# Clustered attention and two MoE layers on one core: the copy's mask in PSUM, V's peak and split in other steps, and attention's last ten steps regrouped

## The chip, the core and the metric

The kernel runs on one core of a Trainium2 chip. The metric is the device time of one execution in microseconds (us), of which the median of several runs is given. The engines are TensorE (PE in the profile, PEld its weight loads), VectorE (DVE), ScalarE (ACT), GpSimd (POOL) and SyncE (SP), which here issues the DMAs.

## The reference

Attention with clusters, 2 batches of 8 heads, 768 tokens, 64 values a head, then two feed-forward layers over 1536 tokens. A query sees a key only where both are nearest to the same of 16 centroids. A query with no key in its cluster has only equal scores, so it gets the mean of V.

```python
q_assign = np.argmax(np.einsum('bhsd,hcd->bhsc', q_n, c_n), axis=-1)
k_assign = np.argmax(np.einsum('bhsd,hcd->bhsc', k_n, c_n), axis=-1)
mask = q_assign[:, :, :, None] == k_assign[:, :, None, :]
scores = np.where(mask, scale * np.matmul(q, k.transpose(0, 1, 3, 2)), -1000000000.0)
attn = np.exp(scores - np.max(scores, axis=-1, keepdims=True))
x = np.matmul(attn / (np.sum(attn, axis=-1, keepdims=True) + 1e-09), v)   # heads side by side: 1536 x 512
...
h = x @ w_in      # 512 -> 2048
g = np.where(h >= 1, h, np.where(h <= -1, 0.0, (h + 1) ** 2 / 4))
x = g @ w_out     # 2048 -> 512
...
h = x @ w2_in
out = (s * np.maximum(h, 0) ** 2 + b) @ w2_out
```

## The kernel before, in words

**Precision by halves.** Products are taken with each operand split in a high part and a low part, so that a product is three matmuls (high by high, low by high, high by low). Every tensor that goes to TensorE has a pair of instructions that splits it: a rounding copy on ScalarE, and a subtraction on VectorE or GpSimd. V is first scaled by a power of two, taken from its largest magnitude, and split in two halves of 16 bits.

**Attention in steps.** The 16 heads are 8 pairs; a head has 6 chunks of 128 keys, which makes NS = 96 steps. `slot(t)` writes one step:

- two matmuls of row maxima (`max_mm`, L722) for chunk t + 9, in two banks of PSUM called m, and VectorE's reduces of them (L733);
- `scores` (L783, L784) of chunk t, in three banks called s, and `probs`: two exponentials a half on ScalarE (L794, L795) and the low half pl by a subtraction (L797) on GpSimd, or on VectorE for the steps that the table VPL names;
- `values` (L813) of chunk t − 2, 18 matmuls into the one bank called o. After a head's sixth chunk `finish` (L824, L828, L831) reads that bank on VectorE, and only then the next head's values can start;
- the pieces that tables have put into step t: `steps` hold triples (TensorE part, ScalarE part, VectorE part) whose TensorE part stands at the end of step t and whose other parts stand in step t + 1; `mid` stands before the step's values, `extra` at its end, `dmas` at its start.

The pieces are the turns of q and k (transposes L483, L492, L496), the clusters (L520 to L565), V's magnitudes (`scale_v`, L595), V's peak (`peak_row` L607 to L617, `peak_all` L628 to L642), V's split (`split_v` on ScalarE, L650; `split_v2` on VectorE, L654), the mean of V (L666 to L672), the row of maxima (`max_row`, L762, L767, and a DMA L771 that the scores of that head need), the stacks that DMAs build from the halves (L683), the replacement of unmatched rows (`no_match`, L838 on ScalarE, then the predicated copy L839 on VectorE) and the transposed output (`x_out`, L855, L860, L863, two pieces a pair). All that need a bank in PSUM take it from the pool x by `spare()`. The pool has two banks, given out by turns, so a piece waits until the readers of the last piece but one are done.

**Order.** Each engine runs its instructions in the order in which the program was written, so the tables set it. With z = 12p for pair p, the table PV gives the steps (relative to z) of V's load, `scale_v`, `peak_row`, `peak_all`, and of the four splits, for even and odd pairs apart. V has one buffer in SBUF (rv), so the load of a pair waits until the last `split_v2` of the pair before has read it. The DMAs queue on SP in order.

**Into the MoE.** After attention 96 units follow, each of twelve matmuls for h (L241), the activation (L254 to L270), the split of g (L275, L277) and twelve matmuls for y (L302) into four banks that `emit_y` names by pools. Their weights arrive as 64-bit numbers and are converted: L134 on ScalarE, four operations on VectorE (L151, L155, L159, L163), then L179 on ScalarE and L180 on GpSimd. The first four pieces of weights are converted in attention's last ten steps, at times that the table EARLY gives (and a pool of the intermediate buffers), and h of the first two units is computed there or right behind (`early_h`).

Of the kernel before, what the change touches and what calls it, by code (L numbers as in the profile page):

```python
# [8 lines left out]
F32 = mybir.dt.float32  # L9
# [16 lines left out]
def clustered_attention_moe_kernel(  # L26
# [29 lines left out]
    J = S // 128  # L56
# [12 lines left out]
    NWA, NWB, NWC, NWD = 2, 5, 7, 2  # L69

    EARLY = (
        (85, 87, 87, 88, 88, 89, "m"), (88, 90, 90, 91, 91, 92, "m"), (91, 93, 93, 94, 94, 95, "x"),
        (95, 98, 98, 99, 99, None, "x"),
    )
    LOADS = (56, 62, 68)
    PACES = ((2, 0.7), (28, 0.9))
    TAIL = 3
    VPL = (87, 90, 93, 95)
    PV = ((-11, -9, (-8, -6), -5, -3, -3, -2), (-13, -11, (-8, -6), -5, -3, -2, 0))
    PX = ((7, 16, 17), (7, 16, 17))  # L80
    PT = (38, 35, 36, 34, 27, 26, 25, 24)
    PG = (23, 22, 20, 18, 17, 16, 14)
    PN = (8, 12, 9)


# [15 lines left out]
    def bank(kind, name):  # L101
        return banks[kind].tile([128, TB], F32, tag=kind, name=name)
# [81 lines left out]
    ff = {"wa": wa}  # L184
# [13 lines left out]
    units = [(m, t, c) for m, t, a, b in RUNS for c in range(a, b)]  # L198
# [16 lines left out]
    def w_free(m, c):  # L215

        x = w_pool(m, c)
        i = SHARES[x].index((m, c)) - {"wa": NWA, "wb": NWB, "wc": NWC, "wd": 0}[x]
        if x == "wd":
            return use2[0, FC - 1] + 1  # L220
        return use2[SHARES[x][i]] if i >= 0 else -2
# [5 lines left out]
    g_t, y_t, h_t = {}, {}, {}  # L227
# [56 lines left out]
    def emit_y(m, t, c):  # L284
        wh, wl = w_t[m, c][:, 0], w_t[m, c][:, 1]
        gh, gl = g_t.pop((m, t, c))
        begin, end = (m, t, c) in BEGIN, (m, t, c) in END
        if begin:
            y_t[m, t] = [bank(x, "y") for x in "mmxo"]
        y = y_t[m, t]  # L290
        order = [(i, n) for n in range(3) for i in range(KD)]
        if begin or end:
            order.sort()
        for i, n in order:
            cs = slice(i * 128, (i + 1) * 128)
            ws = slice(DM + i * 128, DM + (i + 1) * 128)
            wd = slice(DM, 2 * DM)
            if m == 0:
                ops = ((wh[:, ws], gh), (wh[:, ws], gl), (wl[:, ws], gh))
            else:  # L300
                ops = ((gh[:, cs], wh[:, wd]), (gl[:, cs], wh[:, wd]), (gh[:, cs], wl[:, wd]))
            nc.tensor.matmul(  # L302
                y[i], lhsT=ops[n][0], rhs=ops[n][1], start=(begin and n == 0), stop=(end and n == 2)
            )
        if end:
            emit_out(m, t, c, y_t.pop((m, t)))
# [50 lines left out]
    h = 3  # L357
    for n, w in enumerate(loadq[len(early):]):
        start, pace = PACES[w[0]]
        n -= (0, 2 * FC - len(early))[w[0]]  # L360
        h = max(h + 1.4, 2 * (w_free(*w[0:2]) + 3), 2 * (start + pace * n))
# [45 lines left out]
    def attention(es, prep):  # L407
        def pool(name, bufs, stack=es):
            side = "left" if stack is prep else "right"
            return stack.enter_context(tc.tile_pool(name=name, bufs=bufs, side=side))  # L410
# [10 lines left out]
        smp = pool("smp", 4)  # L421
# [23 lines left out]
        def spare():  # L445

            if spares:
                spares.append(spares.pop(0))
                return bank(spares[-1], spares[-1] + "b")
            return bank("x", "xb")  # L450
# [101 lines left out]
        def match(g, n):  # L552

            j0, j1 = PIECE[n]
            cs = slice(j0 * 128, j1 * 128)
            st = {}

            def pe():
                ps = st["ps"] = spare()[:, 0:(j1 - j0) * 128]
                nc.tensor.matmul(ps, lhsT=firsts, rhs=sims[g, "t"][:, cs], start=True, stop=True)  # L560

            def dve():
                if n == 0:
                    ohts[g] = ohp.tile([128, S], F32, tag="oht", name="oht")
                nc.vector.tensor_scalar(  # L565
                    out=ohts[g][:, cs], in0=st["ps"], scalar1=level[:, 0:1], scalar2=level[:, 1:2],
                    op0=ALU.is_gt, op1=ALU.mult,
                )

            return pe, None, dve  # L570
# [218 lines left out]
        def probs(t):  # L789
# [3 lines left out]
            for qs, ps in pr[t]:  # L793
                nc.scalar.activation(out=ph[:, qs], in_=ps, func=ACTF.Exp, scale=qk_scale)  # L794
                nc.scalar.activation(out=pf[:, qs], in_=ps, func=ACTF.Exp, scale=qk_scale)  # L795
            eng = nc.vector if t in VPL else nc.gpsimd
            eng.tensor_tensor(out=pl, in0=pf, in1=ph, op=ALU.subtract)  # L797
# [36 lines left out]

        def no_match(p):

            nm = smp.tile([128, 2, J], F32, tag="nm", name="nm", bufs=2)
            nc.scalar.activation(out=nm, in_=heads.pop((p, "mx")), func=ACTF.Relu, scale=-1.0, bias=low)  # L838
            nc.vector.copy_predicated(  # L839
                out=heads[p, "x"],  # L840
                mask=nm.bitcast(I32).rearrange("p h j -> p j h")[:, :, :, None].to_broadcast([128, J, 2, D]),
                data=vt[p][4][:, None].to_broadcast([128, J, 2, D]),
            )
# [54 lines left out]
        NS = NH * J  # L898
        steps, extra, mid, dmas = {}, {}, {}, {}

        def at(d, t, f, *a):
            d.setdefault(t, []).append((f, a))

        def step(t, x):
            steps.setdefault(t, []).append(x)

        for g in range(1, NH // 4):
            z = 24 * g
            for a, at_load, places in ((0, 46, PT[0:4]), (1, 34, PT[4:8])):
                p = 2 * g + a  # L910
                at(dmas, z - at_load, load_qk, p)
                for o, (nm, n) in zip(places, (("q", 0), ("q", 1), ("k", 0), ("k", 1))):
                    step(z - o, turn(p, nm, n))
            step(z - PG[0], sim(g, 0))
            step(z - PG[1] + int(g == 1), sim(g, 1))
            at(extra, z - PG[2], chain1, g)
            at(extra, z - PG[3], chain2, g)
            at(extra, z - PG[4], chain3, g)
            step(z - PG[5], match(g, 0))
            step(z - PG[6], match(g, 1))  # L920
        for p in range(NP):
            z = 12 * p
            zl, za, zs, zh, zg = PV[p % 2][0:3] + (PV[p % 2][3:5], PV[p % 2][5:7])
            at(dmas, z + zl, load_v, p)
            at(extra, z + za, scale_v, p)
            step(z + zs[0], peak_row(p))
            step(z + zs[1], peak_all(p))
            for e in range(2):
                at(extra, z + zh[e], split_v, p, e)
                at(extra, z + zg[e], split_v2, p, e)  # L930
            zx = PX[p % 2]
            step(z + zx[0], mean(p))
            if p < NP - 1:
                step(z + zx[1], x_out(p, 0))
                step(z + zx[2], x_out(p, 1))
# [11 lines left out]

        def early_h(n, kk):
            if kk == 0:
                ff["h"] = bank("m", "h")  # L950
            emit_h(*units[n], ff["h"], H_PARTS[3 * kk:3 * kk + 3])

        at(extra, 6 * (NH - 1) - 11, ready)
# [9 lines left out]
                at(extra, z[5], conv_split, w)  # L963
        for kk in range(KD):
            at(mid, NS - 5 + kk, early_h, 0, kk)
        at(extra, NS - 1, emit_g, *units[0], True)
        at(extra, NS - 1, emit_g2, *units[0], True)
        at(extra, NS, emit_split, *units[0], False)
        at(mid, NS, early_h, 1, 0)
        at(mid, NS + 1, early_h, 1, 1)  # L970
        at(extra, NS + 1, early_h, 1, 2)
# [164 lines left out]
```

## Time and profile before

| | |
|---|---|
| median of three runs | 797.81 us (797.04 to 799.7) |
| the profiled execution | 798.17 us |
| its span, first to last instruction | 796.5 us |
| mean granted TensorE clock | 0.981 |
| TensorE busy | 752.2 us (94%), 4993 matmuls |
| VectorE busy | 499.5 us (63%) |
| ScalarE busy | 472.7 us (59%) |
| GpSimd busy | 311.2 us (39%) |

A line of a timeline reads: start in us from the span's start, duration in us, engine, line of the kernel, operation, output and inputs by the program's names, sizes; in square brackets how long the engine had been idle before it, and what ended that. A line of the waits reads: the waiting engine and its line, the instruction that ended the waits, the total, how many, the longest. In the windows, the third number from the end is the granted clock, 1.00 being the full one; in front of it stand the busy us of TensorE, its weight loads, VectorE, ScalarE and GpSimd. Busy TensorE is not TensorE at its peak, since matmuls overlap in the pipeline.

### The profile page before, as it was taken

Reading aid. Unit: us, or ns where it says so; the run is one execution under the profiler, and the core shown is the slowest. Engines: PE = TensorE matmul, PEld = TensorE weight load, DVE = VectorE, ACT = ScalarE, POOL = GpSimd, SP = SyncE. Lnnn points to the kernel's source line nnn. Section 1 sums busy time; section 2 is a strip of 40 time slices with the busy share of each in tenths; the row PEclk is TensorE's granted clock in tenths of the full one; section 3 lists DMA queues with packets and bytes.
Section 4 is the critical chain, followed back from the end, with each engine's and each line's share of the span. In section 5 each row is a group of like instructions: output and inputs, shape, how many; then the busy total and the mean of one; then the engine's idle time right before and its main releaser. Section 6 shows DMA issues by size and latency. Waiting matters only on the chain.

```text
span 796.5 us, 13144 instructions
## 1 busy us (share of the span) xinstructions
PE 752.2 (94%) x4993; PEld 629.4 (79%) x4993; DVE 499.5 (63%) x878; ACT 472.7 (59%) x943; POOL 311.2 (39%) x237
## 2 busy tenths in 40 slices
PE   4799998998998799999999999999999999999998
PEld 3488887887886568788888888888888888888886
DVE  5779899898887696888447336879962322222222
ACT  4178968877898477787646425876653333343332
POOL 3057767767885346365405201654560000000000
PEclk9599999999999899999999999999999999999999
DMA  9576566536531144344203100443410100010001
GB/s 199 111 165 148 119 140 137 139 92 150 139 67 54 30 156 133 110 138 149 80 0 110 50 0 30 150 139 101 143 49 0 53 1 0 1 54 0 1 1 53
DMA packets 59887, 67.52 MB, mean 85 GB/s; under 512 B 29008, under 2 KB 47536, under 8 KB 59824
## 3 DMA queue, kind: packets, MB, share of 16 engines
q1 hardware_dynamic: 59824, 66.68, 31.8%
q8 instruction: 39, 0.64, 0.3%
q14 instruction: 24, 0.20, 0.1%
HBM read 43.03 MB, written 3.15 MB: 58 GB/s over the span
## 4 chain that ended last, share of the span: by engine, by line
PE 79%; DVE 14%; ACT 4%; issue 1%; DMA 0%; DVEq 0%; ACTq 0%
PE y L302 31%; PE h L241 30%; PE m L722 4%; PE o L813 4%; PE s L783 3%; PE s L784 3%; DVE rowmax L733 3%; PE xb L520 2%; DVE x L839 1%; PE xb L483 1%; DVE c L151 1%; PE xb L855 1%; DVE c L155 1%; DVE c L159 1%; DVE rowmax L754 1%
## 5 line engine op out<-in xcount | busy, mean ns | idle before, releaser
L241 PE MATMUL h<-xt_h,w 128*128 128x512 f32 x768 | 253.3, 391 | 1.7 <-ACT w L179 1.7
L797 POOL TENSOR_TENSOR pl<-pf,ph 128x768 f16<-128x768 f32 x92 | 155.3, 1693 | 93.8 <-ACT pf L795 71.1
L241 PEld LDWEIGHTS h<-xt_h,w 128*128 128x128 f32 x768 | 144.4, 188 | 32.2 <-ACT w L179 2.1
L241 PE MATMUL h<-xt_l,w 128*128 128x512 f32 x384 | 149.8, 390 | 0.0
L277 POOL TENSOR_TENSOR gl<-g,gh 128x512 fp32r<-128x512 f32 x51 | 66.8, 1310 | 187.1 <-ACT gh L275 187.1
L275 ACT ACTIVATE gh<-g 128x512 fp32r<-128x512 f32 x96 | 60.5, 630 | 108.3 <-PE y L302 66.7
L794 ACT ACTIVATE ph<-s 128x384 f16<-128x384 f32 x192 | 98.8, 515 | 32.7 <-PE s L784 31.1
L302 PE MATMUL y<-gh,w 128*128 128x512 f32 x384 | 109.8, 394 | 4.2 <-DVE g L268 2.8
L733 DVE TENSOR_REDUCE rowmax<-m 128x1 f32<-128x384 f32 x180 | 95.4, 549 | 24.2 <-PE m L722 23.0
L302 PE MATMUL y<-w,gh 128*128 128x512 f32 x384 | 105.3, 389 | 0.0
L795 ACT ACTIVATE pf<-s 128x384 f32<-128x384 f32 x192 | 100.2, 522 | 0.0
L270 DVE TENSOR_SCALAR g<-g,cols 128x512 f32<-128x512 f32 x48 | 27.4, 571 | 100.8 <-ACT g L261 100.6
L302 PEld LDWEIGHTS y<-gh,w 128*128 128x128 f32 x384 | 72.9, 190 | 20.9 <-DVE g L268 3.2
L180 POOL TENSOR_TENSOR w<-t,w 128x512 fp32r<-128x512 f32 x64 | 83.4, 1315 | 1.7 <-ACT w L179 1.7
L302 PEld LDWEIGHTS y<-w,gh 128*128 128x128 f32 x384 | 72.1, 188 | 15.0
L241 PEld LDWEIGHTS h<-xt_l,w 128*128 128x128 f32 x384 | 72.3, 188 | 14.6
L722 PE MATMUL m<-kb,qb 80*128 80x384 f32 x180 | 70.4, 395 | 7.3 <-DVE rowmax L733 6.9
L260 ACT ACTIVATE g<-h 128x512 f32<-128x512 f32 x48 | 28.6, 596 | 78.3 <-PE h L241 76.5
L813 PEld LDWEIGHTS <-ph 128*128 128x128 f16 x1152 | 55.2, 98 | 21.6 <-issue 13.4
L277 DVE TENSOR_TENSOR gl<-g,gh 128x512 fp32r<-128x512 f32 x45 | 31.2, 693 | 62.5 <-ACT gh L275 62.5
L813 PE MATMUL o<-vh,ph 128*128 128x65 f16 x576 | 63.9, 197 | 4.0 <-DVE x L831 3.8
L783 PE MATMUL s<-qa,ka 128*128 128x384 f32 x192 | 66.9, 349 | 0.0
(164 smaller groups left out, 1317.1 us busy)
## 6 DMA issues: line engine op xcount, KB each, us to landing
raw<-in_moe_w_in_dram SPq DMA_DIRECT2D x32, 512.0 KB, 5.2
raw<-in_moe_w_out_dram SPq DMA_DIRECT2D x32, 512.0 KB, 3.5
rq<-in_q_dram SPq DMA_DIRECT2D x16, 192.0 KB, 4.4
rk<-in_k_dram SPq DMA_DIRECT2D x16, 192.0 KB, 4.2
rv<-in_v_dram SPq DMA_DIRECT2D x8, 384.0 KB
qb<-qh SPq DMA_DIRECT2D x16, 192.0 KB, 4.0
kb<-kh SPq DMA_DIRECT2D x16, 192.0 KB, 3.1
qa<-qh SPq DMA_DIRECT2D x16, 192.0 KB, 3.0
```

What stands on the lines that cost most here:

```text
L180: nc.gpsimd.tensor_tensor(out=l, in0=f, in1=h.bitcast(F32), op=ALU.subtract)
L241: nc.tensor.matmul(h_t[m, t, c], lhsT=w[:, kk * 128:(kk + 1) * 128], rhs=x[:, kk, tokens(t)], start=((n, kk) == H_PARTS[0]), stop=((n, kk) ...
L275: nc.scalar.activation(out=gh, in_=g, func=ACTF.Copy)
L277: eng.tensor_tensor(out=gl, in0=g, in1=gh.bitcast(F32), op=ALU.subtract)
L302: nc.tensor.matmul(y[i], lhsT=ops[n][0], rhs=ops[n][1], start=(begin and n == 0), stop=(end and n == 2))
L722: nc.tensor.matmul(ps, lhsT=hd["qb"][0:NQ, j * 128:(j + 1) * 128], rhs=hd["kb"][0:NQ, n * S // 2:(n + 1) * S // 2], start=True, stop=True,)
L733: nc.vector.tensor_reduce(out=hd["m2"][:, j, n:n + 1], in_=mst.pop((u, n)), axis=AX.X, op=ALU.max)
L783: nc.tensor.matmul(ps, lhsT=hd["ka"][:, cs], rhs=hd["qa"][:, qs], start=True, stop=False)
L794: nc.scalar.activation(out=ph[:, qs], in_=ps, func=ACTF.Exp, scale=qk_scale)
L795: nc.scalar.activation(out=pf[:, qs], in_=ps, func=ACTF.Exp, scale=qk_scale)
L797: eng.tensor_tensor(out=pl, in0=pf, in1=ph, op=ALU.subtract)
L813: nc.tensor.matmul(o[:, j, 0:w], lhsT=lhsT[:, js], rhs=rhs[:, e, c, :], start=(c == 0 and j == 0 and x == 0), stop=(c == J - 1 and j == J ...
```

## The change

The mask of `no_match` is written into a bank of the pool x instead of a tile in SBUF. The steps of V's load, magnitudes, peak and splits shift: for even pairs magnitudes and all later pieces come one or two steps later; for odd pairs the load comes one step later, the magnitudes stand in `mid` instead of `extra` (for pair 1 at step 4), and the peak and the splits are moved together. The load of pair 1, which the part ahead of step 0 issues anyway, is no longer in the table. One piece of the clusters (chain2) comes a step later. In the last ten steps two of four subtractions for pl go back to GpSimd, the conversions of the first weights get other steps, h of the second unit takes a bank of the pool s, the second and third bank of y change places, and the activation of the first unit is written one step earlier.

```diff
--- before.py
+++ after.py
@@ -69,17 +69,17 @@
     NWA, NWB, NWC, NWD = 2, 5, 7, 2
 
     EARLY = (
-        (85, 87, 87, 88, 88, 89, "m"), (88, 90, 90, 91, 91, 92, "m"), (91, 93, 93, 94, 94, 95, "x"),
-        (95, 98, 98, 99, 99, None, "x"),
+        (86, 88, 88, 89, 89, 90, "m"), (89, 90, 90, 91, 91, 93, "m"), (92, 93, 93, 94, 94, 96, "x"),
+        (94, 96, 96, 96, 96, None, "x"),
     )
     LOADS = (56, 62, 68)
     PACES = ((2, 0.7), (28, 0.9))
     TAIL = 3
-    VPL = (87, 90, 93, 95)
-    PV = ((-11, -9, (-8, -6), -5, -3, -3, -2), (-13, -11, (-8, -6), -5, -3, -2, 0))
+    VPL = (93, 95)
+    PV = ((-11, -8, (-6, -4), -3, -2, -2, -1), (-12, -11, (-6, -5), -3, -2, -2, -1))
     PX = ((7, 16, 17), (7, 16, 17))
     PT = (38, 35, 36, 34, 27, 26, 25, 24)
-    PG = (23, 22, 20, 18, 17, 16, 14)
+    PG = (23, 22, 20, 19, 17, 16, 14)
     PN = (8, 12, 9)
 
 
@@ -286,7 +286,7 @@
         gh, gl = g_t.pop((m, t, c))
         begin, end = (m, t, c) in BEGIN, (m, t, c) in END
         if begin:
-            y_t[m, t] = [bank(x, "y") for x in "mmxo"]
+            y_t[m, t] = [bank(x, "y") for x in "mxom"]
         y = y_t[m, t]
         order = [(i, n) for n in range(3) for i in range(KD)]
         if begin or end:
@@ -834,7 +834,7 @@
 
         def no_match(p):
 
-            nm = smp.tile([128, 2, J], F32, tag="nm", name="nm", bufs=2)
+            nm = spare()[:, 0:2 * J].rearrange("p (h j) -> p h j", h=2)
             nc.scalar.activation(out=nm, in_=heads.pop((p, "mx")), func=ACTF.Relu, scale=-1.0, bias=low)
             nc.vector.copy_predicated(
                 out=heads[p, "x"],
@@ -921,8 +921,9 @@
         for p in range(NP):
             z = 12 * p
             zl, za, zs, zh, zg = PV[p % 2][0:3] + (PV[p % 2][3:5], PV[p % 2][5:7])
-            at(dmas, z + zl, load_v, p)
-            at(extra, z + za, scale_v, p)
+            if p != 1:
+                at(dmas, z + zl, load_v, p)
+            at(*((extra, z - 8) if p == 1 else (mid if p % 2 else extra, z + za)), scale_v, p)
             step(z + zs[0], peak_row(p))
             step(z + zs[1], peak_all(p))
             for e in range(2):
@@ -947,7 +948,7 @@
 
         def early_h(n, kk):
             if kk == 0:
-                ff["h"] = bank("m", "h")
+                ff["h"] = bank("ms"[n], "h")
             emit_h(*units[n], ff["h"], H_PARTS[3 * kk:3 * kk + 3])
 
         at(extra, 6 * (NH - 1) - 11, ready)
@@ -963,9 +964,9 @@
                 at(extra, z[5], conv_split, w)
         for kk in range(KD):
             at(mid, NS - 5 + kk, early_h, 0, kk)
-        at(extra, NS - 1, emit_g, *units[0], True)
-        at(extra, NS - 1, emit_g2, *units[0], True)
-        at(extra, NS, emit_split, *units[0], False)
+        at(extra, NS - 2, emit_g, *units[0], True)
+        at(extra, NS - 2, emit_g2, *units[0], True)
+        at(extra, NS - 1, emit_split, *units[0], False)
         at(mid, NS, early_h, 1, 0)
         at(mid, NS + 1, early_h, 1, 1)
         at(extra, NS + 1, early_h, 1, 2)
```

The first place is VectorE in steps 40 to 42, where pair 2's output pieces (L863) stand beside V's peak of pair 4 (L611 to L642). Before:

```order
L863 TENSOR_TENSOR xt_l<-xb,xt_h 128x512
L611 TENSOR_REDUCE pk<-xb 2x1
L614 TENSOR_SCALAR ex<-pk 2x1
L617 TENSOR_SCALAR ex<-ex 2x1
L733 TENSOR_REDUCE rowmax_2420<-m 128x1 x2
L863 TENSOR_TENSOR xt_l<-xb,xt_h 128x256
L733 TENSOR_REDUCE rowmax_2420<-m 128x1 x2
L638 TENSOR_SCALAR sc<-xb 128x2
L642 COPY iv<-xb 128x2
L824 TENSOR_SCALAR rd<-o,sc 128x6
L828 RECIPROCAL rd<-rd 128x6
```

and now:

```order
L863 TENSOR_TENSOR xt_l<-xb,xt_h 128x512
L733 TENSOR_REDUCE rowmax_2420<-m 128x1 x2
L863 TENSOR_TENSOR xt_l<-xb,xt_h 128x256
L733 TENSOR_REDUCE rowmax_2420<-m 128x1 x2
L611 TENSOR_REDUCE pk<-xb 2x1
L614 TENSOR_SCALAR ex<-pk 2x1
L617 TENSOR_SCALAR ex<-ex 2x1
L824 TENSOR_SCALAR rd<-o,sc 128x6
L828 RECIPROCAL rd<-rd 128x6
L831 TENSOR_TENSOR x<-o,rd 128x6x64
```

The peak no longer stands between the two output pieces, but two reduces behind them, and its second part (L638, L642) has gone into the next head's reduces. TensorE's transposes for these pieces, L855 and L607, have moved in the same way.

The second place is VectorE in steps 86 to 88, from the copy of pair 6 (L839) on; mr (L767) is the row that a DMA takes to the scores of the last head. Before:

```order
L839 COPY_PREDICATED x<-nm,mv 128x768
L797 TENSOR_TENSOR pl<-pf,ph 128x768
L151 TENSOR_SCALAR c<-t 128x512
L155 TENSOR_SCALAR c<-c 128x512
L767 TENSOR_SCALAR mr<-xb 6x128
L159 SCALAR_TENSOR_TENSOR c<-raw,c 128x512
```

and now:

```order
L839 COPY_PREDICATED x<-xb,mv 128x768
L767 TENSOR_SCALAR mr<-xb 6x128
L151 TENSOR_SCALAR c<-t 128x512
L155 TENSOR_SCALAR c<-c 128x512
L863 TENSOR_TENSOR xt_l<-xb,xt_h 128x512
L159 SCALAR_TENSOR_TENSOR c<-raw,c 128x512
```

The subtraction L797 is gone from there (it is on GpSimd), and mr follows the copy at once.

The third place is VectorE a little later, up to the finish of head 14 (L824 to L831). Before:

```order
L863 TENSOR_TENSOR xt_l<-xb,xt_h 128x512
L797 TENSOR_TENSOR pl<-pf,ph 128x768
L863 TENSOR_TENSOR xt_l<-xb,xt_h 128x256
L151 TENSOR_SCALAR c<-t 128x512
L155 TENSOR_SCALAR c<-c 128x512
L159 SCALAR_TENSOR_TENSOR c<-raw,c 128x512
L163 SCALAR_TENSOR_TENSOR t<-raw,c 128x512
L824 TENSOR_SCALAR rd<-o,sc 128x6
L828 RECIPROCAL rd<-rd 128x6
L831 TENSOR_TENSOR x<-o,rd 128x6x64
```

and now:

```order
L863 TENSOR_TENSOR xt_l<-xb,xt_h 128x256
L151 TENSOR_SCALAR c<-t 128x512
L155 TENSOR_SCALAR c<-c 128x512
L159 SCALAR_TENSOR_TENSOR c<-raw,c 128x512
L163 SCALAR_TENSOR_TENSOR t<-raw,c 128x512
L824 TENSOR_SCALAR rd<-o,sc 128x6
L828 RECIPROCAL rd<-rd 128x6
L831 TENSOR_TENSOR x<-o,rd 128x6x64
```

One subtraction less stands ahead of the finish, and the output piece L863 of 512 values has gone further up; the conversion is where it was.

## Rows read from the trace of the kernel before

**Rows 1.** The page, busy time: engine, busy us, share of the span, instructions.

```profile
PE 752.2 (94%) x4993; PEld 629.4 (79%) x4993; DVE 499.5 (63%) x878; ACT 472.7 (59%) x943; POOL 311.2 (39%) x237
```

**Rows 2.** Chain that ended last: start us, length us, engine, tile, line, instructions.

```profile
269.54 4.21 PE y L302 x9
...
327.65 2.72 PE y L302 x12
```

**Rows 3.** Waits of TensorE, 40 to 290 us: who, total us, times, longest.

```profile
PE m L722 <- DVE rowmax L733: 6.3, 7, 1.7
PE xb L855 <- DVE xt_l L863: 4.6, 6, 0.8
PE o L813 <- DVE x L831: 3.8, 7, 1.7
PE y L302 <- DVE g L268: 2.8, 1, 2.8
PE h L241 <- ACT w L179: 1.7, 1, 1.7
PE s L784 <- DMA qb<-mr: 1.2, 1, 1.2
PE y L302 <- POOL gl L277: 0.8, 1, 0.8
PE y L302 <- ACT gh L275: 0.8, 1, 0.8
```

**Rows 4.** Windows: stretch, busy us and instructions by engine, granted clock, DMA share, GB/s.

```profile
186.00:192.00 6.00, 4.34 (x49) 3.67 (x49) 5.40 (x8) 3.52 (x10) 4.04 (x4) 0.82 0.68 197
270.00:276.00 6.00, 6.00 (x19) 4.71 (x19) 0.73 (x2) 1.12 (x2) 0.17 (x1) 0.57 0.00 0
```

**Rows 5.** Timeline of TensorE: first rowmax matmul of steps 40, 41, 64, 65.

```profile
133.59 0.45 PE L722 MATMUL m<-kb,qb 80*128 80x384 f32 x1 [1.26 <-DVE rowmax L733]
...
135.90 0.45 PE L722 MATMUL m<-kb,qb 80*128 80x384 f32 x1
...
189.21 0.45 PE L722 MATMUL m<-kb,qb 80*128 80x384 f32 x1 [1.66 <-DVE rowmax L733]
...
192.76 0.65 PE L722 MATMUL m<-kb,qb 80*128 80x384 f32 x1
```

**Rows 6.** By line: VectorE duration ns min/median/max, first and last start, forms.

```profile
L839 DVE COPY_PREDICATED x<-nm,mv x8: 1845/2293/2455, 74.6 to 265.0; 128x768 f32<-128x768 int32 x8
...
L654 DVE SCALAR_TENSOR_TENSOR vl<-rv,sc,vh x16: 596/995/1375, 40.1 to 235.1; 128x384 f16<-128x384 f32 x16
...
L831 DVE TENSOR_TENSOR x<-o,rd x16: 556/557/558, 60.7 to 264.3; 128x384 f32<-128x384 f32 x16
```

**Rows 7.** Timeline, VectorE and GpSimd, around the copy of step 38.

```profile
130.62 0.41 DVE L496 TENSOR_TENSOR ql<-xb,qh 128x256 fp32r<-128x256 f32 x1
130.95 2.14 DVE L839 COPY_PREDICATED x<-nm,mv 128x768 f32<-128x768 int32 x1
...
130.58 1.65 POOL L797 TENSOR_TENSOR pl<-pf,ph 128x768 f16<-128x768 f32 x1 [0.24 <-ACT pf L795]
```

**Rows 8.** Lines by shape: busy us, mean ns, idle time before and its releaser.

```profile
L650 ACT ACTIVATE vh<-rv,sc 128x384 f16<-128x384 f32 x16 | 10.1, 636 | 2.5 <-DVE sc L638 2.5
...
L838 ACT ACTIVATE nm<-rowmax,cols 128x12 f32<-128x12 f32 x8 | 2.6, 326 | 0.0
```

**Rows 9.** Timeline: V's load on its queue, and the reader on VectorE, steps 24 to 25 and 72 to 73.

```profile
93.87 0.38 SPq L468 DMA_DIRECT2D rv<-in_v_dram  x1
...
99.44 0.95 DVE L595 TENSOR_REDUCE ab<-rv 128x2 f32<-128x768 f32 x1 [0.63 <-DMA rv<-in_v_dram]
...
206.98 0.38 SPq L468 DMA_DIRECT2D rv<-in_v_dram  x1
...
210.99 0.94 DVE L595 TENSOR_REDUCE ab<-rv 128x2 f32<-128x768 f32 x1
```

**Rows 10.** Timeline of VectorE, passage to the MoE: the row of maxima for the last head.

```profile
244.22 0.27 DVE L767 TENSOR_SCALAR mr<-xb 6x128 fp32r<-6x128 f32 x1
```

## The prediction

> **What bounds the kernel now.** I read the page's busy shares first: TensorE is busy 94% of the span [rows 1]. Then the chain that ended last: from about 290 us on it is TensorE alone, twelve matmuls of y and twelve of h by turns, 2.72 us each, up to the end [rows 2]. The change touches none of them, so whatever it does must come out of the first 290 us, where attention and the first units of the MoE lie. There TensorE has hardly any slack either, so the third view is what it waits for between 40 and 290 us: the eight largest kinds make 22.0 us [rows 3]. The first three lie mostly in attention's steps, the other five in the passage from attention to the MoE. A hole of TensorE is worth its length here, since nothing behind it can catch up.
>
> Some holes cost twice. Behind the longest wait for a rowmax (1.66 us at 189.21) the granted clock is 0.82 in 186 to 192 us, and behind the holes of the passage it is 0.57 in 270 to 276 us [rows 4, 5], that is partly at 1.2 GHz instead of 2.4.
>
> The sum is made against the profiled execution: 798.17 us, of which the span is 796.5, so 1.7 us lies around it. The median of the runs is 797.81, 0.36 less. About 0.3% (2.4 us) is what a measurement of this kernel can tell from no change.
>
> **Part 1: the mask in PSUM.** The predicated copy takes 1.85 to 2.46 us [rows 6]. The one at 130.95 us starts under a subtraction of GpSimd that ends at 132.23 (130.58 + 1.65) and itself ends at 133.09, 0.86 us behind it [rows 7]. So it seems to stand still while GpSimd works and to need some 0.9 by itself. Two neighbours on VectorE say the same: L654 reads two SBUF tensors and takes 596 to 1375 ns for 384 elements; L831 reads one from PSUM and one from SBUF and takes 556 to 558 ns in all 16 cases [rows 6]. L831 is the changed copy's nearest row, with half its elements. 384 more at some 1.04 ns (the copy's own pace of 0.86 us over 768, at most 1.12 ns) add 0.4: 0.96 us. Bounds: 0.86 (what ran behind GpSimd) and 2.46 (nothing gained). I take 0.96, which is 1.29 less than the mean of 2.25.
>
> *The Trainium skill, "SBUF — State Buffer", section "Who interferes with whom", says that a VectorE instruction with two SBUF inputs contends with a GpSimd instruction that reads SBUF, and one with at most one SBUF input does not. By it the copy is freed, unless the old output, which it keeps where the mask is zero, counts as an input too; then two remain and nothing is gained, which is rival 1.*
>
> Behind the copy VectorE has the reduces for which TensorE waits, 6.3 us in seven waits [rows 3]. Of these 1.26 stands ahead of each of steps 16 and 40 and 1.66 ahead of step 64 [rows 5]; the other 2.1 follow the copies of steps 26, 50 and 74, and the shorter copy takes them away: 2.0. In the first three the mask now needs one of the pool's two banks, and the one it gets is freed by ql (L496), which ends at 131.03, where the copy started at 130.95 [rows 7]. With nm's own 0.33 [rows 8] and the handing over, the copy starts 0.5 later, and the exponentials queued behind nm on ScalarE some 0.65. So only 1.29 − 0.65 = 0.64 each: 1.9. Together **3.9**.
>
> With the wait of 1.66 down to 1.0 I expect the clock to hold there. Step 64 took 3.55 us (189.21 to 192.76), its like, step 40, took 2.31 (133.59 to 135.90) [rows 5]: **1.2**.
>
> **Part 2: V's peak behind the output transposes.** The second output transpose of a pair waits 0.77 us for L863 of the first, six times, 4.6 us [rows 3], because peak_row (L607) took a bank between them. Now peak_row comes two steps later (first order piece) and each transpose has a bank: **4.6** gone. What is late next there is ScalarE's copy of the first piece, which has a step's time. Values wait for finish (L831) 3.8 us, 1.7 of it in the passage; the other 2.1 stand in six places right behind late reduces and go with them but for some 0.2: **1.9**.
>
> Against it stands V's load. It leaves when the last split_v2 of the pair before has read the single buffer. That is one step, some 2 us, later before odd pairs, while the magnitudes (L595) keep their step. Before, the load left at 93.87 and L595 started at 99.44, after 0.63 of waiting for it; in step 73 it left at 206.98 and L595 started at 210.99 without a wait [rows 9]. So it lands within 5.6 us in the one case and at most 4.0 in the other. Left 2 us later, it makes VectorE stand still for about 0.63 + 1.5 = 2.1 in step 25 (L595 itself is a little later) and some 1.4 in each of steps 49 and 73: 4.9. Queued behind L595 are finish and the reduces that TensorE waits for, so I pass all of it on: **−4.9**. Bounds: 0 (the true landing is earlier than the reader's start shows) and −8 (every load takes 5.6).
>
> ScalarE's part of the split (0.64 us a piece [rows 8]) moves into steps that hold a turn besides the four exponentials; of it some 0.4 for an even pair and 0.2 for an odd one can't be hidden: 3 × 0.6, **−1.8**; bounds 0 and −3.8 (six whole pieces). chain2 and peak_all, moved by a step or two, cost nothing: their readers follow a step or more behind.
>
> Main part: 3.9 + 1.2 + 4.6 + 1.9 − 4.9 − 1.8 = **4.9**.
>
> **Part 3: the last ten steps.** Before, a copy, a subtraction and two conversions stand ahead of mr on VectorE, so it starts at 244.22 [rows 10] and the scores wait 1.2 for its DMA. Now it follows the copy at once (second order piece), and the wait goes. Before, a subtraction and four conversions hold up finish, for which values wait 1.7: two subtractions go to GpSimd, where one takes 1.65 [rows 7] and a step is longer than that, and finish comes in time. The waits of y(0) for its two halves (0.8 and 0.8) go, since g is a step earlier, but the subtraction left in step 95 then holds the last values for about 1.0. The wait of 2.8 for L268 was for the bank that held h of unit 1; h now lies in another pool, and what is left is the o bank, freed by the last finish behind a conversion: 0.3. The wait of 1.7 for L179 shrinks to about 0.75, since the late copy and the late g no longer stand ahead of the conversions. Nine matmuls of y took 4.21 us on the slow clock, at 2.72 / 12 each they take 2.04 [rows 2]; with the transposes and first h behind them, some 0.8, the slow clock cost 3.0.
> 1.2 + 1.7 + 0.8 + 0.8 + 2.8 + 1.7 + 3.0 = 12.0, less 1.0 + 0.3 + 0.75: **9.9**. Bounds: 6 (the clock falls all the same, GpSimd a little late) and 11.
>
> **Total:** 4.9 + 9.9 = 14.8; 798.17 − 14.8 = 783.4, in round figures 783 us.
>
> **Rivals.**
> 1. *The copy gets no shorter*, because its output is a second SBUF input; no row shows a predicated copy free of GpSimd. Part 1's 3.9, the clock's 1.2 and the 1.9 of values go, and the bank's 0.65 counts against it three times: 14.8 − 9.0 = 5.8, so 792. Against it: the 0.86 behind GpSimd's end fits a wait for the mask. Chance 0.13.
> 2. *The clock falls at the passage and in step 64, and the load takes its bound*: 3.0 + 1.2 + 3.1 less, 791. For it: the hole before the last values stays. Chance 0.15.
> 3. *VectorE's and ScalarE's new delays are absorbed*: 4.9 and 1.8 come back, 777. For it: L595's wait before (0.63) is in none of TensorE's rows. Chance 0.14.
> 4. *Slower: the mask's bank.* From nm's start to the copy's end one of the two banks is held; the turns, transposes and max_row (L762) share the other, and VectorE does nothing else. If twelve mask values read 64 times each out of PSUM make the copy long, each of seven copies costs TensorE its excess over 0.96. It decides from (14.8 + 2.4) / 7 = 2.5 of excess on, a copy of 3.4 us: 801 and more. Against it: L831 from PSUM needs 1.45 ns an element, 1.1 us for 768. Chance 0.06.
>
> **How the numbers follow.** My forecast has 0.52, with a range of its own of 779 to 788. With rivals 2 and 3 that is 0.81, and 776 to 792 holds them and the near part of rival 1. Over 795.4 lie rival 4 and a tail of rivals 1 and 2 with Part 3 at its bound: same 0.06, slower 0.07, faster 0.87.
>
> **What would show it.** Right: copies near 0.96 us, never stretched under GpSimd; no wait of L855 on L863; VectorE waiting 1 to 2 us for V's load in steps 25, 49 and 73; a clock of 1.00 from the last step on; the regular turns of y and h about 15 us sooner. Wrong: a copy of 2 us; TensorE waiting for the mask's bank; values waiting for GpSimd's subtractions in the last ten steps; a clock near 0.5 behind them.

## The result, and the profile after

The changed kernel takes 784.59 us (median of 4 runs, 782.97 to 785.35) where the kernel before takes 798.15 (4 runs, 797.04 to 799.7). The ratio is 0.9826, 95% interval 0.9803 to 0.9849: some 13.6 us faster. The prediction said 783, range 776 to 792.

The page of the changed kernel (span, busy time, and the granted clock in 40 slices):

```profile
span 782.9 us, 13151 instructions
...
PE 750.2 (96%) x4993; PEld 627.1 (80%) x4993; DVE 486.7 (62%) x876; ACT 471.7 (60%) x943; POOL 312.0 (40%) x239
...
PEclk9589999999899999999999999999999999999999
```

TensorE lost 13.6 us of span and only 2.0 of busy time (752.2 before [rows 1]): what went was waiting. Its waits between 40 and 290 us, the view of [rows 3], make 10.2 us now where the eight largest kinds alone made 22.0:

```profile
PE o L813 <- DVE x L831: 3.3, 6, 2.1
PE m L722 <- DVE rowmax L733: 2.1, 3, 1.1
PE h L241 <- ACT w L179: 1.2, 2, 0.7
PE m L722 <- DMA kb<-oht: 1.1, 1, 1.1
PE s L783 <- ACT pf L795: 0.9, 2, 0.7
PE o L813 <- DVE pl L797: 0.7, 1, 0.7
PE xb L762 <- DVE x L839: 0.7, 2, 0.3
```

The waits for L863 (4.6) and L268 (2.8) are gone, and those for the reduces have fallen from 6.3 to 2.1. New are a wait for a DMA (kb from oht), two of scores for the exponentials (L795) that still read their bank, and two of max_row (L762) for the copy that now holds a bank. The copy by line, as in [rows 6]:

```profile
L839 DVE COPY_PREDICATED x<-xb,mv x8: 1000/1034/1040, 77.7 to 259.4; 128x768 f32<-128x768 int32 x8
```

All eight copies take 1.00 to 1.04 us, whether GpSimd works beside them or not.

To place the 13.6 us I took, in the traces of both, the time of the first score matmul of each step and of the first h matmul of the fifth unit. Before, these two rows are the start of step 86 and that matmul:

```profile
236.91 0.34 PE L783 MATMUL s<-qa,ka 128*128 128x384 f32 x1
...
285.08 0.50 PE L241 MATMUL h<-xt_h,w 128*128 128x512 f32 x1 [1.69 <-ACT w L179]
```

and these in the changed kernel, with a third row that is spoken of below:

```profile
232.17 0.34 PE L783 MATMUL s<-qa,ka 128*128 128x384 f32 x1
...
270.49 0.50 PE L241 MATMUL h<-xt_h,w 128*128 128x512 f32 x1 [0.51 <-ACT w L179]
...
309.02 0.50 PE L302 MATMUL y<-gh,w 128*128 128x512 f32 x1 [1.34 <-DVE t L163]
```

| stretch | predicted gain, us | in the two traces, us |
|---|---|---|
| steps behind the copies (15, 16, 27, 28, 39, 40, 51, 52, 63, 64), clock included | 3.9 + 1.2 | 6.6 |
| steps of the output transposes and the peak (17 to 20, 29, 30, and their likes) | 4.6 + 1.9 | 6.1 |
| V's load: steps 25 and 49; steps 74 to 76 | −4.9 | 0; −3.9 |
| other steps (ScalarE's split and the rest) | −1.8 | −1.5 |
| steps 5 to 8 | none | −1.9 |
| step 0 to step 86 | 4.9 | 5.4 |
| step 86 to the fifth unit's h (48.17 before, 38.32 now) | 9.9 | 9.85 |
| from there to the end (511.38, 512.41) | 0 | −1.0 |
| ahead of step 0, where the first score matmul comes at 39.62 and 40.33 | 0 | −0.7 |

The last line is no effect of the change: in the fourteen traces of this study, whose work up to there is all but the same, that start lies between 39.6 and 41.1.

### The profile page after: what moved, and what is told of

Read it like the earlier page. It is cut to its first block, busy times and chain, and to the rows that moved or that the text cites. A ratio compares the mean times of both kernels' runs of the same rounds, so it can differ in the third digit from the quotient of the medians.

```text
span 782.9 us, 13151 instructions
## 1 busy us (share of the span) xinstructions
PE 750.2 (96%) x4993; PEld 627.1 (80%) x4993; DVE 486.7 (62%) x876; ACT 471.7 (60%) x943; POOL 312.0 (40%) x239
## 4 chain that ended last, share of the span: by engine, by line
PE 83%; DVE 9%; ACT 5%; issue 1%; DMA 1%; SPq 0%; DVEq 0%; ACTq 0%
PE y L302 31%; PE h L241 30%; PE o L813 5%; PE m L722 4%; PE s L783 3%; PE s L784 3%; PE xb L520 2%; DVE rowmax L733 1%; PE xb L483 1%; ACT ph L794 1%; ACT pf L795 1%; DVE rowmax L754 1%; DVE c L155 1%; DVE c L159 1%; DMA kb<-oht 1%
## 5 line engine op out<-in xcount | busy, mean ns | idle before, releaser
L797 POOL TENSOR_TENSOR pl<-pf,ph 128x768 f16<-128x768 f32 x94 | 156.2, 1666 | 84.8 <-ACT pf L795 55.4
L794 ACT ACTIVATE ph<-s 128x384 f16<-128x384 f32 x192 | 101.5, 529 | 27.3 <-PE s L784 26.2
L795 ACT ACTIVATE pf<-s 128x384 f32<-128x384 f32 x192 | 102.9, 536 | 0.0
```

## The experiments

Each was compared with the kernel before on the same chip; times are medians. The kernel before took 798.15 to 799.24 us in these comparisons, so a difference to the changed kernel's 784.59, which comes from another of them, is uncertain by about 1 us. Where less than that is argued, the steps in the traces decide: outside steps 74 to 76 and a few others, an unchanged step takes the same to about 0.05 us from trace to trace. Three runs made the three parts of the change one by one.

**The mask alone.**

```diff
-            nm = smp.tile([128, 2, J], F32, tag="nm", name="nm", bufs=2)
+            nm = spare()[:, 0:2 * J].rearrange("p (h j) -> p h j", h=2)
```

> The kernel before with the mask in PSUM and nothing else. Theory (the sum's Part 1): the copies take 1.00 to 1.04 us as in the changed kernel, the waits of TensorE for the reduces behind them shrink from 6.3 us in all to some 2.5, the clock stays at 1.00 around 190 us, and the six waits of 0.77 for L863 stay: about 5 us faster, 793. Rival (the copy's time is only worth something together with V's new places, because peak_row now finds one bank less): the banks take back what the copy gives, waits of TensorE on turns or on peak_row appear in the steps behind each copy, and the time stays within 1 us of 798.

793.81 against 798.82, ratio 0.9934 (0.9917 to 0.9952): 5.0 us, where the sum had 5.1. Its waits of TensorE, 40 to 290 us:

```profile
PE xb L855 <- DVE xt_l L863: 4.6, 6, 0.8
...
PE m L722 <- DVE rowmax L733: 0.6, 3, 0.2
PE xb L607 <- DVE mr L767: 0.5, 1, 0.5
```

The reduces are hardly waited for any more (0.6 of 6.3, where 2.5 was expected), the waits for L863 stay. The rival's wait on a bank shows once (L607, 0.5): step 64, where that transpose stands, takes 3.34 us with the clock at 1.00, and 2.10 in the changed kernel, where the transpose has moved away. It is not what decides. The theory holds.

**V's pieces alone** (the tables PV and PG and the loop over pairs as in the change, all else as before).

> The kernel before with V's load, magnitudes, peak, splits and chain2 in the new steps, and nothing else. Theory: the six waits of 0.77 for L863 go (4.6 us), against which stand 1.8 us in steps 5 to 7 (magnitudes of pair 1 in step 4), some 2 us of the splits among the turns, and the late load of the last pair with what follows from it in steps 73 to 76 (4 to 5 us with the clock): 798 to 802, so same or slower. Rival (the sum's Part 2 as predicted, 4.6 + 1.9 - 4.9 - 1.8 with losses of equal size in steps 25, 49 and 73): VectorE waits for the load by 1 us or more in all three steps and the time is near 798.

797.92 against 798.82, ratio 0.9987 (0.9976 to 0.9999), so 0.9 us. The six waits for L863 are gone. Steps 5 to 8 lose 1.8 and steps 74 to 76 3.4, while steps 25 and 49 are as long as before to 0.02 us. VectorE waits 0.86, 0.83 and 1.38 us for the load in the three steps, not 1 us or more in all. The time (near 798) fits both; the steps decide for the theory. This run also shows a copy with both inputs in SBUF at a time when GpSimd does nothing (the last copy but two; timeline of VectorE and of GpSimd):

```profile
212.18 1.00 DVE L839 COPY_PREDICATED x<-nm,mv 128x768 f32<-128x768 int32 x1
...
205.38 1.65 POOL L797 TENSOR_TENSOR pl<-pf,ph 128x768 f16<-128x768 f32 x1 [0.37 <-PE m L722]
...
215.90 1.65 POOL L797 TENSOR_TENSOR pl<-pf,ph 128x768 f16<-128x768 f32 x1 [4.01 <-ACT pf L795]
```

GpSimd stops at 211.88 and starts again at 215.90; the copy between takes 1.00 us.

**The last ten steps alone** (EARLY, VPL, the banks of h and y, g a step earlier; mask and V's pieces as before).

> The kernel before with the changes of the last ten steps alone (two subtractions back on GpSimd, times of the conversions, banks of h and y, g a step earlier), mask in SBUF and V's pieces where they were. Theory: these hang on nothing else, so the passage gains what it does in the changed kernel, 8 to 9 us: 789.5, with the clock at 1.00 behind the last step. Rival: without the short copy, the copy of pair 6 (2.4 us, longer beside GpSimd, which has more to do now) still delays the row of maxima and the last one the bank of y; then 3 us or more are missing, and the time is 792 or above.

790.44 against 798.82, ratio 0.9898 (0.9878 to 0.9918): 8.4 us. From step 86 to the fifth unit's h it takes 38.33 us, the same as the whole change (38.32), with the long copy. So the passage does not need the short copy. The three parts measure 5.0 + 0.9 + 8.4 = 14.3; together they gave 13.6. They add up within what the runs scatter.

**The other input in PSUM.** The mask is back in SBUF, the mean of V goes through a bank.

```diff
-            nm = spare()[:, 0:2 * J].rearrange("p (h j) -> p h j", h=2)
+            nm = smp.tile([128, 2, J], F32, tag="nm", name="nm", bufs=2)
+            mv = spare()[:, 0:2 * D].rearrange("p (h d) -> p h d", h=2)
...
+            nc.scalar.activation(out=mv, in_=vt[p][4], func=ACTF.Copy)
...
-                data=vt[p][4][:, None].to_broadcast([128, J, 2, D]),
+                data=mv[:, None].to_broadcast([128, J, 2, D]),
```

> The changed kernel with the mask back in SBUF and the other input, the mean of V, in PSUM instead (ScalarE copies it into the bank that held the mask, one more instruction of ScalarE for each pair). Theory (two inputs in SBUF meet GpSimd on a shared way; it does not matter which one leaves): the copies take 1.0 to 1.1 us, whether or not GpSimd works. Rival (it is the mask, twelve values read 64 times each out of SBUF): they take 1.8 to 2.5 us as before.

The copy by line:

```profile
L841 DVE COPY_PREDICATED x<-nm,xb x8: 998/1026/1048, 78.1 to 260.3; 128x768 f32<-128x768 int32 x8
```

The same 1.0 us, and 785.58 in the one run. It does not matter which input leaves SBUF; that the mask is read 64 times a value is not the cost.

**The load of the last pair.** In the changed kernel it leaves SP at 201.03; here are its reader on VectorE (L595), the finish queued behind it, and the matmul that waits for the stack (timeline by engine):

```profile
201.03 0.38 SPq L468 DMA_DIRECT2D rv<-in_v_dram  x1
...
204.64 0.95 DVE L595 TENSOR_REDUCE ab<-rv 128x2 f32<-128x768 f32 x1 [1.20 <-DMA rv<-in_v_dram]
...
205.98 0.56 DVE L831 TENSOR_TENSOR x<-o,rd 128x384 f32<-128x384 f32 x1
...
208.38 0.66 PE L722 MATMUL m<-kb,qb 80*128 80x384 f32 x1 [1.07 <-DMA kb<-oht]
```

VectorE stands still 1.20 us for the load, values wait 2.06 for finish (the longest in the first row of the waits above), and then TensorE waits 1.07 for a piece of the stack that left SP behind the load. The windows there (columns as in [rows 4]) show TensorE busy for 2.87 us of 6 and the clock at 0.80, then 0.63:

```profile
204.00:210.00 6.00, 2.87 (x27) 2.47 (x26) 4.40 (x9) 2.08 (x6) 3.45 (x3) 0.80 0.89 189
210.00:216.00 6.00, 6.00 (x56) 5.26 (x54) 2.51 (x5) 3.81 (x10) 3.02 (x2) 0.63 0.00 1
```

Two theories: the reader, or what stands behind the load on SP. First the magnitudes alone, three steps later:

```diff
-            at(*((extra, z - 8) if p == 1 else (mid if p % 2 else extra, z + za)), scale_v, p)
+            at(*((extra, z - 8) if p in (1, 7) else (mid if p % 2 else extra, z + za)), scale_v, p)
```

> The changed kernel with the magnitudes of the last pair three steps later (step 76), the load and its queue untouched. Theory 1 (VectorE's wait for V's load in step 73, and finish queued behind it, is what makes steps 74 to 76 4 us longer): the wait of 2.06 for finish goes, and the clock stays: 3 to 4 us faster, 781. Theory 2 (the stack's DMAs queue behind the load on SP, and kb from oht lands at 208.3 whatever VectorE does, while TensorE would want it near 205.3): the wait of 2.06 goes and the one for kb from oht grows from 1.07 to about 3, so the time stays within 1 us of 784.6.

783.79: 0.8 less than the changed kernel, within what such a difference can tell. Its largest wait of TensorE:

```profile
PE m L722 <- DMA kb<-oht: 2.8, 1, 2.8
```

The wait for finish went, and the one for the DMA grew from 1.07 to 2.8: theory 2. Then the load behind the stack as well:

```diff
-                at(dmas, z + zl, load_v, p)
+                at(dmas, z + zl + (p == 7), load_v, p)
```

> As the run with the last pair's magnitudes later, and V's load of the last pair issued one step later too, so that the eight DMAs of the stack go out ahead of it. Theory 2 (the late load costs by what stands behind it on SP, and by its reader on VectorE): both waits go, steps 74 to 76 together take some 7 us instead of 11.7 and the clock stays at 1.00 from 204 to 216 us: 4 us faster than the changed kernel, 780.5. Theory 1: no more than with the magnitudes alone.

779.31, which is 5.3 below the changed kernel. Steps 74 to 76 take 6.3 us (11.7 in the changed kernel, 7.8 before), and the windows are

```profile
204.00:210.00 6.00, 5.67 (x77) 4.83 (x77) 5.36 (x12) 5.17 (x15) 5.25 (x4) 1.00 0.63 154
210.00:216.00 6.00, 6.00 (x89) 5.40 (x87) 5.12 (x14) 5.80 (x16) 5.12 (x4) 1.00 0.61 134
```

Moving the reader alone had not helped, and the clock is at 1.00 now. The load behind the stack with its reader left in step 73 was not run, so it is shown that the order on SP is needed, not that the reader's move is. Nor do all of the 5.4 us between 11.7 and 6.3 come with every execution: in the five runs that follow, whose steps 74 to 76 are written as in the changed kernel, they take 10.0 to 10.4 us (step 76, for one, 2.1 to 2.7 instead of 3.2), so against those traces the edit is worth 3.7 to 4.1.

**Steps 5 to 8.** The section on the change says that chain2 comes a step later. It comes a step earlier: PG counts back from a pair's first step, and with 19 for 18 the first placed group's chain2 moves from step 6 to step 5. In the changed kernel VectorE has, in a row, the magnitudes of pair 1 and chain2 (L543, 1.80 us beside GpSimd), and TensorE waits for the reduces behind each (timeline of VectorE and of TensorE):

```profile
55.45 0.94 DVE L595 TENSOR_REDUCE ab<-rv 128x2 f32<-128x768 f32 x1
...
57.24 1.80 DVE L543 TENSOR_TENSOR eq<-sim,mx 128x768 f16<-128x768 f32 x1
...
56.92 0.44 PE L722 MATMUL m<-kb,qb 80*128 80x384 f32 x1 [1.05 <-DVE rowmax L733]
...
59.56 0.45 PE L722 MATMUL m<-kb,qb 80*128 80x384 f32 x1 [0.66 <-DVE rowmax L733]
```

Pair 1 as before, chain2 left in its new step:

```diff
-            zl, za, zs, zh, zg = PV[p % 2][0:3] + (PV[p % 2][3:5], PV[p % 2][5:7])
+            x = (-13, -11, (-8, -6), -5, -3, -2, 0) if p == 1 else PV[p % 2]
+            zl, za, zs, zh, zg = x[0:3] + (x[3:5], x[5:7])
...
-            at(*((extra, z - 8) if p == 1 else (mid if p % 2 else extra, z + za)), scale_v, p)
+            at(*((extra, z + za) if p == 1 else (mid if p % 2 else extra, z + za)), scale_v, p)
```

> The changed kernel with the pieces of pair 1 alone in the steps that they had before (magnitudes in step 1, peak in 4 and 6, splits from 7 on); chain2 stays in its new step. Theory (magnitudes in step 4 fall on VectorE beside the first cluster pieces and hold up the reduces for steps 6 and 7): the waits of 1.05 and 0.66 there go, steps 5 to 8 take 8.7 instead of 10.6 us, and the kernel is 1.5 to 1.9 us faster, 782.9. Rival (chain2, one step earlier there, does it): the waits stay, and so does the time.

784.4, no gain. Steps 5 to 8 take 10.2 us (10.6 in the changed kernel, 8.7 before), and one wait of 1.38 stands ahead of the matmul of step 7, behind an L543 that is longer still (timeline of VectorE and of TensorE):

```profile
58.49 2.15 DVE L543 TENSOR_TENSOR eq<-sim,mx 128x768 f16<-128x768 f32 x1
...
61.17 0.44 PE L722 MATMUL m<-kb,qb 80*128 80x384 f32 x1 [1.38 <-DVE rowmax L733]
```

L543 reads two inputs in SBUF. GpSimd works beside it for 1.77 us here, and for 0.19 us in the next run, where it takes 0.95. My theory fell. So chain2 alone:

```diff
-            at(extra, z - PG[3], chain2, g)
+            at(extra, z - PG[3] + int(g == 1), chain2, g)
```

> The changed kernel with chain2 (the comparison L543) of the first placed group back in step 6; pair 1 keeps its new steps. After the run with pair 1 put back, where steps 5 to 8 stayed long, theory: it is L543, 1.8 us beside GpSimd in step 5, that holds up the reduces; steps 5 to 8 go from 10.6 to about 9 us and the kernel gains 1.3 to 1.9 us, 782.9. Rival (either of the two pieces is enough to fill VectorE there): steps 5 to 8 keep 10 us or more, and the gain is under 0.6.

782.89; steps 5 to 8 take 9.7. The steps give 0.8 of the 1.7 us that the medians differ by, and steps 74 to 76, which the edit does not touch, are 1.3 shorter in this trace, so the time is the theory's by chance. Neither theory nor rival holds as it was put: each piece alone is enough to lose about 1 to 1.4 us there, and only both put back can give the 1.9, which the last run shows.

**The banks of h and y.**

```diff
-            y_t[m, t] = [bank(x, "y") for x in "mxom"]
+            y_t[m, t] = [bank(x, "y") for x in "mmxo"]
...
-                ff["h"] = bank("ms"[n], "h")
+                ff["h"] = bank("m", "h")
```

> The changed kernel with the banks of h of the second unit and of y as before, everything else of the last ten steps new. Theory (the hole of 2.8 us ahead of y's second bank, and the slow clock behind it, come from the bank that h of unit 1 holds until VectorE has read it): a wait of 2 to 3 us of y for L268 comes back; the clock behind it falls (below 0.9 in a 6 us window) and with it the loss is 3.5 to 5.5 us, 788 to 790. Rival (the earlier g and the freed VectorE give that bank back in time anyway): the wait is under 1 us, the clock stays, 784.5 to 785.5.

788.46, 3.9 more than the changed kernel. The wait is back, and the clock falls behind it:

```profile
PE y L302 <- DVE g L268: 3.2, 1, 3.2
```

```profile
258.00:264.00 6.00, 3.50 (x8) 2.81 (x9) 2.30 (x4) 0.29 (x1) 0.00 (x0) 0.63 0.30 87
```

From step 86 to the fifth unit's h it takes 43.65 us against 38.32: 5.3 of the 9.85 hang on the banks. Then y's order alone (the first of the two edits):

> The changed kernel with y's banks in the order of before (both m, then x, then o); h of the second unit stays in the pool s. Theory (moving h alone frees the second m bank; the order of y's banks is not needed for that, and it costs at the next run of units, where the bank from x is now wanted three matmuls earlier and TensorE waits 1.34 us instead of 0.31): no wait of y for L268 comes back, the wait of 1.34 shrinks to 0.3 to 0.7, and the kernel is about 1 us faster, 783.5. Rival (both parts are needed): a wait of 1 us or more at the first y, 786 or above.

783.27, 1.3 less, with 37.97 us of passage. In the traces 0.35 of that is in the passage and 0.7 behind it. No wait for L268, and the wait of 1.34 at 309.02 is

```profile
PE y L302 <- DVE t L163: 0.7, 1, 0.7
```

So h's pool does it all. The new order of y only makes the x bank wanted three matmuls earlier where the next run of units begins. (The order is not an exchange of the second and the third bank, as the section on the change has it: the second m goes to the end, and x and o each move up a place.)

**Four subtractions on VectorE.**

```diff
-    VPL = (93, 95)
+    VPL = (87, 90, 93, 95)
```

> The changed kernel with four subtractions of pl on VectorE as before (steps 87, 90, 93, 95 instead of 93, 95). Theory (Part 3): the one of step 87 stands between the copy and the row of maxima again and the one of step 90 ahead of finish; with the short copy each costs less than before, but values wait for finish by 0.5 to 1 us and steps 88 to 93 are 1 to 2 us longer: 785.6 to 786.6. Rival (the short copy alone had already made room on VectorE, and the two on GpSimd only move work from one busy engine to another): within 0.5 us of 784.6, or faster because the waits of scores for the exponentials' buffer (0.9) go.

784.15, within the scatter of the changed kernel, so by the time it is the rival that holds. In the traces the passage is 0.95 us longer (39.27), as the waits for the row of maxima and for finish are back in part (0.48 and 0.91), while those of the scores for the exponentials are shorter (0.5 for 0.9) and 0.3 comes back later. So the waits are in the theory's places, with a smaller sum.

**What was given back, together:** the edits of the load, of pair 1, of chain2 and of y's order.

> The changed kernel with what the runs above gave back: V's load of the last pair behind the stack and its magnitudes in step 76, the pieces of pair 1 and chain2 of the first placed group in the steps of before, y's banks in the order of before. Theory (the three losses are separate: 5.2 us measured at steps 73 to 76, 1.9 read from steps 5 to 8, 1.0 at y's banks): 784.6 - 8.1 = 776.5, steps 5 to 8 8.7 us, no wait for kb from oht, the wait of y for L163 at most 0.7. Rival (they overlap, as waits of the same engines further on): 778 to 779.

776.44 (5 runs, 776.21 to 776.87) against 799.24, ratio 0.9715 (0.97 to 0.9731): 8.15 below the changed kernel's 784.59, where 8.1 was expected (each taken from its own comparison's kernel before, the two gain 22.8 and 13.6, 9.2 apart; the spans of the two traces are 8.4 apart). Its waits of TensorE, 40 to 320 us, the four largest:

```profile
PE o L813 <- DVE x L831: 1.2, 5, 0.3
PE h L241 <- ACT w L179: 1.1, 2, 0.7
PE s L783 <- ACT pf L795: 0.9, 2, 0.7
PE m L722 <- DVE rowmax L733: 0.9, 3, 0.4
```

The losses were separate: steps 5 to 8 take 8.8 us, steps 74 to 76 6.3. No wait between 40 and 320 us is over 0.7 us any more.

## Why the prediction was right

**The copy (0.96 us, 0.86 to 2.46).** 1.00 to 1.04 in all eight. The nearest row, L831, gave it within 0.08. Rival 1 (the output counts as an input) falls by two runs: with the mask in PSUM and with the mean in PSUM the copy takes 1.0 beside a working GpSimd. The copy with both in SBUF while GpSimd stood still takes 1.0 as well, which shows that the long copies were long because of GpSimd; it does not tell the rival from the theory. *The rule that I cited from the Trainium skill, "SBUF — State Buffer", "Who interferes with whom", agrees: with one SBUF input no copy of the changed kernel is over 1.04, with two they took up to 2.46.* Part 1 by itself measured 5.0 of 5.1 predicted, and its pieces came out too: with the mask alone, steps 15 and 16 gain 0.69, 39 and 40 0.56 (0.64 each in the sum), and 63 and 64 1.83 (0.64 and the clock's 1.2). The 6.6 of the table is more because steps 16, 40 and 64 also gain from the peak's transpose that left them: V's pieces alone give 0.23, 0.21 and 1.66 there. The last number bears on the clock's term: in that run, with the long copy and a wait of 1.75 ahead of step 64, the clock was at 1.00 too. So it is not shown that the clock came back because of the copy.

**The transposes (4.6 + 1.9).** All six waits for L863 went, and the steps concerned gained 6.1. But 1.4 of that is moved work: two matmuls of the peak (L628) left steps 30, 54 and 78 for 31, 55 and 79, which are longer by as much and stand in the table's row of other steps. What is left, 4.7, is the transposes. The 1.9 of values' waits for finish did not come. Five of those six waits made 1.4 and still make 1.2 (3.3 less the 2.1 of step 74, and the first row of the last run above); the sixth, in step 74, was

```profile
212.94 0.20 PE L813 MATMUL o<-vh,ph 128*128 128x65 f16 x1 [0.77 <-DVE x L831]
```

before, and went up to 2.06. They do not end with the late reduces, as I had it.

**V's load (−4.9): the term that failed most.** The step was "Queued behind L595 are finish and the reduces that TensorE waits for, so I pass all of it on". In steps 25 and 49 TensorE has twelve matmuls of the clusters to do, so VectorE's wait lies beside them. The chain of the changed kernel has, in this order, these matmuls at step 25 and the DMA at step 73:

```profile
99.36 2.84 PE xb L520 x12
...
203.34 4.91 DMA kb<-oht
```

and the reader in step 25 waits 0.73, not 2.1 (timeline of VectorE):

```profile
100.46 0.95 DVE L595 TENSOR_REDUCE ab<-rv 128x2 f32<-128x768 f32 x1 [0.73 <-DMA rv<-in_v_dram]
```

Step 25 takes 4.51 us, before 4.48. In step 73 there are no such matmuls. There I had priced the reader (1.4; it waited 1.20), and not the stack behind the load on SP: kb from oht left 203.34 and landed 4.91 later. Put right, the load costs what the run with the stack ahead gained: 5.3 by the medians, 3.7 to 5.4 by the steps of the traces. So −4.9 was near the total by chance: nothing in two places, and about three to four times the price in the third.

**Steps 5 to 8 (no term).** "chain2 and peak_all, moved by a step or two, cost nothing" was wrong in the first placed group: with the magnitudes of pair 1 it cost 1.9. The reason given, that the readers follow later, leaves out the reduces that queue on VectorE behind a piece that has come earlier. I had not looked at the first pairs, which have steps of their own.

**ScalarE's split (−1.8).** The steps in which the splits now stand (34 and 45 to 47, for example) take the same as before within 0.03. The 1.5 that the other steps lose is the peak's two matmuls in steps 31, 55 and 79 (1.4, as above). Of the rest, steps 12, 36, 60, 72 and 84 lose 1.3 and the remaining steps gain as much (61, 70 and 83 alone 0.9); so the −1.8 came out near 0.

**The passage (9.9).** 9.85 was measured. Of it, 5.3 is the bank of h with the clock behind it (the sum had 2.8 + 3.0 for these, less 0.3). Of what I expected to be left (2.05), the last values' wait is 0.65 and L179's 0.51; not foreseen are another wait for L179 (0.66) and the scores' waits for L795 (0.9). The two subtractions are worth about 1 us in the passage and nothing in the medians, not the 2.9 of the two waits that I put down to them; they were not needed for most of it. How the rest divides between the conversions' times and the earlier g was not tried. The sum assumed nothing behind the passage, and 1.0 was lost there, in the wait for L163 (1.34, before 0.3); y's old order gives 0.7 of it back.

So the copy, the six waits for L863 and the bank of h were right as mechanisms, and they carry most of the gain. That the total came out within 1.6 us is in part luck. The sum had too much gain for finish's waits (by 1.7), for steps 5 to 8 (1.9) and behind the passage (1.0), and too little for ScalarE's split (1.8) and the steps behind the copies (1.5); and the load was near its sum for another reason than the one given.

## What to carry to other kernels

- A VectorE instruction with two inputs in SBUF that stands beside GpSimd is a candidate for one input in PSUM, even one of twelve values; which of the two doesn't matter, and the price is a bank from the write to the read.
- When a load moves on a queue, price what queues behind it as well as its reader, and ask in each step what TensorE has to do meanwhile: the same change cost nothing in two steps and some 4 to 5 us in the third.
- If a bank is the cause of a hole, move its holder; changing the order of those who want it may only shift the wait to the next place where the order is used.

## What was not expected of the hardware

The clock does not fall behind every hole of the same size. Ahead of step 64 TensorE waits 1.66 us before and 1.75 us in the run with V's pieces alone; the granted clock of the 6 us that hold the hole is 0.82 in the one [rows 4] and 1.00 in the other (timeline of TensorE, and the window):

```profile
188.59 0.44 PE L722 MATMUL m<-kb,qb 80*128 80x384 f32 x1 [1.75 <-DVE rowmax L733]
...
186.00:192.00 6.00, 4.25 (x59) 3.70 (x59) 5.54 (x8) 3.90 (x11) 4.17 (x3) 1.00 0.62 182
```

Step 76 took 3.18 us in the changed kernel and 2.08 in the run with the banks as before, with holes of 2.1 and 1.1 us ahead of it in the one and 2.2 and 0.6 in the other. So about 1 us of such a price may be there or not.

A small DMA of the stack (16 rows from oht) took 4.91 us to land behind V's load; over the kernel the landings that the trace gives for this kind take 2.5 to 4.9, median 3.3.
